# Attention, a capacity-bound top-k and eight experts on one core: the start, the number lookups and the rounds put in other places

## The chip, the cores and the metric

One Trainium2 chip, of which one core is used. The metric is the device time of one execution in microseconds (us). A profile is one more execution, with its instructions and transfers recorded; its span is a little under its time. In the profile PE (or TensorE) does matrix products and transpositions, PEld its weight loads, DVE is VectorE, ACT is ScalarE, POOL is GpSimd, and SP only issues transfers (DMA). "SPq" marks such an issue.

## The reference

```python
q_n, k_n = rmsnorm(q, g_q), rmsnorm(k, g_k)          # 8 batches, 12 heads, 448 tokens, 64 wide
attn = softmax(q_n @ k_n.T / 8)
x = (attn @ v), heads side by side                    # 3584 tokens x 768
logits = x @ w_gate                                   # 8 experts
expert_idx = argmax(logits); gate_w = softmax(logits) at expert_idx
for e in range(8):
    tok_idx = tokens of expert e, the 80 with the largest gate_w
    out[tok_idx] = gate_w[tok_idx] * (relu(x[tok_idx] @ w1[e]) @ w2[e])   # 768 -> 1024 -> 768
```

All other rows of `out` are zero.

## The kernel before

**Pairs.** The work of attention goes by pairs of heads: 6 pairs a batch, 48 in all. One loop runs n from -4 to 51 (L437), and each engine executes its instructions in the order in which this loop issues them. In round n, pair n+4 is loaded on SP (`load_qk`; its 3 buffers are free again when the pair before in the buffer has been normalised), pair n+3 is squared on ScalarE and summed on VectorE, and POOL raises the mean to the power -0.5 (`square`, `rstd`), pair n+2 is multiplied by it (`normalise`, on POOL), pair n+1 is transposed (`transp`), pair n's scores and their exponentials are made (`score`), pair n-1 gets its product with v and the sums of its probabilities on VectorE (`av`, `presum`), pair n-2 is stored as rows of x in DRAM (`xout`, xr_scratch). "Pair n" below stands for "round n of this loop". Every third pair a part of the expert weights is fetched or put into DRAM as bf16 by POOL's queue (`fetch_w1`, `stage_w`, wb_scratch).

**Gate.** When a batch is done, its logits are turned (`gate1` to `gate3`, pairs 6b+7 and 6b+8), and each expert's best 80 tokens are sought by `rounds`: ten rounds of three VectorE instructions (the eight largest, their places, and their removal). This is done in three lists and a last one: batches 0 to 3 together (queued at pair 27), then these with batches 4 and 5 (pair 39), then with batch 6 (pair 45), and batch 7 after the loop. `lists` stores the candidates' token numbers in a table in DRAM (tab_scratch), and `numbers` looks up, for the 80 that stay, which tokens they were: `place` makes table positions on POOL and has TensorE transpose them, `fetch` looks up 80 numbers for one expert by an indirect DMA on POOL, 8 times, and `store` writes the 640 numbers back into the table for the next list.

**The background queue.** Rounds, lists and lookups of a batch are entries with a cost in one list, `queue`; at the end of each pair `work` takes entries until a budget of 4.2 is used up:

```python
def work(us):
    while queue and us > 0:
        cost, f = queue.pop(0)
        f()
        us -= cost
...
return ([(0.3, place)] + [(0.5, lambda e=e: fetch(e)) for e in range(E)]
        + [(0.0, store)])
```

A round costs 1.9 (448 columns), 1.5 (320), 1.2 (240) or 2.1 (528) there.

**The end.** Behind the loop the weights of experts 4 and 5 are loaded (L502), batch 7's ten rounds run, the four results are merged (L510 to L529; `old` reads the numbers of the third list), and for each expert its 80 rows are gathered (`gather`, POOL, three ahead), scaled and transposed (`xpose`), multiplied by both weights and scattered into `out` (L591).

**The start.** Ahead of the first load, SP issues four loads of the norms' weights and six of the gate's (L74, L75, L91).

Of the kernel before, what the change touches and what calls it, by code (L numbers as in the profile page):

```python
# [9 lines left out]
F32 = mybir.dt.float32  # L10
BF16 = mybir.dt.bfloat16
AF = mybir.ActivationFunctionType
# [8 lines left out]
def kernel(  # L21
# [13 lines left out]
    nc = tc.nc  # L35
# [30 lines left out]

    ident = cpool.tile([128, 128], F32, name="ident")
# [5 lines left out]
    for half in range(2):  # L73
        nc.sync.dma_start(out=gk2[half * D:(half + 1) * D, 0:1], in_=g_q[:, None])  # L74
        nc.sync.dma_start(out=gk2[half * D:(half + 1) * D, 1:2], in_=g_k[:, None])  # L75
# [13 lines left out]
    for hh in range(2):  # L89
        for i in range(NG):  # L90
            nc.sync.dma_start(  # L91
                out=wgs[hh * D:(hh + 1) * D, 4 * i + hh:4 * i + hh + 3:2, 8 * i:8 * i + 8],
                in_=wg_v[hh, :, i])
# [21 lines left out]
    nc.sync.dma_start(out=tab_dram[:, 2, CAP:], in_=cand["c"][:, CAP:].bitcast(U32))  # L115
# [36 lines left out]
    with tc.tile_pool(name="qk", bufs=3) as qkpool, \  # L152
# [44 lines left out]
        def normalise(n, a):  # L197
            if a == 0:
                st[n]["qn"] = prep.tile([ST, 2, NT, 2, D], F32, tag="qn", name="qn")
            qk, rs, qn = st[n]["qk"], st[n]["rs"], st[n]["qn"]  # L200
            nc.gpsimd.tensor_mul(  # L201
                qn[:, a].rearrange("p j h d -> p h j d"),
                qk[:, a].rearrange("p h (j d) -> p h j d", d=D),
                rs[:, a].unsqueeze(3).to_broadcast([ST, 2, NT, D]))
# [165 lines left out]
        def numbers(idx, lev, res):  # L370

            add = tpool.tile([CAP, E], U32, tag="add", name="add")

            def place():
                pf = tpool.tile([E, CAP], F32, tag="pf", name="pf")
                nc.gpsimd.tensor_scalar(pf[:, :], idx[:, :], tabF[:, :], float(lev * LT),
                                        op0=ALU.add, op1=ALU.add)
                tp = tpps.tile([128, 512], F32, tag="tp", name="tpn")
                nc.tensor.transpose(tp[:CAP, :E], pf[:, :], ident[:E, :E])
                nc.vector.tensor_copy(add[:, :], tp[:CAP, :E])  # L380
# [7 lines left out]
            def store():  # L388
                if lev < 2:
                    nc.sync.dma_start(out=tab_dram[:, lev + 1, :CAP].rearrange("e s -> s e"),  # L390
                                      in_=res[:, :])
            return ([(0.3, place)] + [(0.5, lambda e=e: fetch(e)) for e in range(E)]
                    + [(0.0, store)])
# [28 lines left out]
        bg[3] += r + numbers(i, 0, num3)  # L422
# [3 lines left out]
        bg[5] += r + numbers(i, 1, num5)  # L426
        r, i = rounds(lambda: cand["c"][:, :], E, LT, best)
        bg[6] = r + numbers(i, 2, num6)
        queue = []

        def work(us):
            while queue and us > 0:
                cost, f = queue.pop(0)
                f()
                us -= cost

        for n in range(-4, NP + 4):  # L437
            if ok(n + 4):
                load_qk(n + 4)
            if ok(n + 2):  # L440
                load_v(n + 2)
            if 4 <= n < 4 + N // 128:
                i = n - 4
                nc.sync.dma_start(out=out[i * 128:(i + 1) * 128, :], in_=zeros[:, :])
# [47 lines left out]
            work(4.2)  # L492
# [10 lines left out]


    v7 = tpool.tile([E, CAP], F32, name="v7")
    last, lidx = rounds(lambda: gst[B - 1]["R"], E, S, v7)
    for cost, f in last:
        f()
    fin = tpool.tile([E, 3, CAP], F32, name="fin")
# [21 lines left out]
    xgs, xts = {}, {}  # L531

    def gather(e):
        xg = mpool.tile([CAP, XW], F32, tag="xg", name="xg", bufs=3)
        nc.gpsimd.memset(xg[:, :], 0.0)
# [24 lines left out]
    for e in range(E):  # L560
# [28 lines left out]
        if e + 3 < E:  # L589
            gather(e + 3)  # L590
# [40 lines left out]
```

## Time and profile before

| | us |
|---|---|
| median of 3 runs (595.93 to 596.67) | 596.28 |
| the profiled execution | 595.21 |
| its span | 593.3 |
| PE busy in it | 496.1 (84%) |
| DVE busy | 379.5 (64%) |
| POOL busy | 354.4 (60%) |
| ACT busy | 322.3 (54%) |

The shares are means over stages that differ: the start, pairs without and with rounds beside them, the last list, and the experts. What bounds a stage is read from the timeline of that stage and from the waits in it. In a timeline row the first number is the start in us from the beginning of the span, the second the time from the first to the end of the last of its x instructions; in brackets stands how long the engine had been idle and what it waited for.

### The profile page before, as it was taken

Reading aid. Unit: us, or ns where it says so; the run is one execution under the profiler, and the core shown is the slowest. Engines: PE = TensorE matmul, PEld = TensorE weight load, DVE = VectorE, ACT = ScalarE, POOL = GpSimd, SP = SyncE. Lnnn points to the kernel's source line nnn. Section 1 sums busy time; section 2 is a strip of 40 time slices with the busy share of each in tenths; the row PEclk is TensorE's granted clock in tenths of the full one; section 3 lists DMA queues with packets and bytes.
Section 4 is the critical chain, followed back from the end, with each engine's and each line's share of the span. In section 5 each row is a group of like instructions: output and inputs, shape, how many; then the busy total and the mean of one; then the engine's idle time right before and its main releaser. Section 6 shows DMA issues by size and latency. Waiting matters only on the chain. (4 is left out here: it accounts for less than half of the span.)

```text
span 593.3 us, 8594 instructions
## 1 busy us (share of the span) xinstructions
PE 496.1 (84%) x3110; PEld 217.9 (37%) x3110; DVE 379.5 (64%) x644; ACT 322.3 (54%) x457; POOL 354.4 (60%) x285
## 2 busy tenths in 40 slices
PE   0699999999999999999987699399997995005795
PEld 0334344434343443344433233144432432004673
DVE  2375647544654555478979952258979999793442
ACT  1577676776677676777745553466663662000110
POOL 1999956877588488564644787347465570324341
PEclk9999999999999999999997979699997998556998
DMA  4339788795969697977947608958654519834931
GB/s 109 95 94 215 187 229 160 214 216 161 257 159 254 145 251 170 255 155 220 206 149 156 152 21 99 146 102 194 151 129 105 112 34 136 310 132 151 379 116 50
DMA packets 84761, 97.55 MB, mean 164 GB/s; under 512 B 11240, under 2 KB 73200, under 8 KB 83696
## 3 DMA queue, kind: packets, MB, share of 16 engines
q1 hardware_dynamic: 68336, 67.88, 39.7%
q0 software_dynamic: 16384, 29.14, 28.1%
q8 instruction: 24, 0.39, 0.3%
q14 instruction: 17, 0.14, 0.1%
HBM read 97.97 MB, written 36.78 MB: 227 GB/s over the span
## 5 line engine op out<-in xcount | busy, mean ns | idle before, releaser
L228 ACT ACTIVATE at<-ps 112x896 f32<-112x896 f32 x192 | 166.4, 918 | 63.0 <-PE ps L224 43.0
L224 PE MATMUL ps<-qkT 64*112 64x448 f32 x768 | 177.1, 582 | 2.8 <-ACT at L228 2.1
L234 PE MATMUL po<-at,vt 112*64 112x448 f32 x768 | 168.2, 560 | 0.1
L193 POOL TENSOR_TENSOR rs<-ms,nhalf 112x16 f32<-112x16 f32 x48 | 143.7, 2994 | 4.0
L190 POOL TENSOR_SCALAR ms<-ssq 112x16 f32<-112x16 f32 x48 | 26.8, 557 | 150.7 <-DVE ssq L187 149.8
L201 POOL TENSOR_TENSOR qn<-qk,rs 112x512 f32<-112x512 f32 x96 | 112.2, 1196 | 2.7
L187 DVE TENSOR_REDUCE ssq<-sq 112x16 f32<-112x1024 f32 x48 | 58.3, 1215 | 81.5 <-ACT sq L181 78.8
L234 PEld LDWEIGHTS po<-at,vt 112*64 112x64 f32 x768 | 47.5, 138 | 112.3 <-issue 102.7
L224 PEld LDWEIGHTS ps<-qkT 64*112 64x112 f32 x768 | 62.7, 178 | 61.0 <-issue 36.6
L244 DVE TENSOR_TENSOR t<-at 112x896 f32<-112x896 f32 x48 | 53.0, 1105 | 30.4 <-ACT at L228 30.3
L209 PE MATMUL tp<-ident,qn 112*128 112x112 f32 x384 | 49.4, 272 | 20.0 <-POOL qn L201 19.3
L181 ACT ACTIVATE sq<-qk 112x1024 f32<-112x1024 f32 x48 | 50.7, 1057 | 27.2 <-DMA qk<-in_k_dram 24.6
L245 DVE TENSOR_TENSOR sm<-sm,t 112x896 f32<-112x896 f32 x48 | 59.0, 1228 | 1.6
L209 PEld LDWEIGHTS tp<-ident,qn 112*128 112x128 f32 x384 | 38.5, 144 | 55.3 <-POOL qn L201 34.6
L214 ACT ACTIVATE qkT<-tp,gqk 128x448 f32<-128x448 f32 x48 | 30.3, 631 | 43.5 <-PE tp L209 38.8
L243 DVE TENSOR_TENSOR sm<-at 112x896 f32<-112x896 f32 x48 | 53.4, 1112 | 0.0
L572 ACT ACTIVATE h_sb<-ph 128x320 bf16<-128x320 f32 x16 | 6.9, 437 | 72.8 <-PE ph L568 72.8
L250 ACT COPY us<-po 128x448 f32<-128x448 f32 x48 | 25.7, 534 | 25.4 <-PE po L234 24.7
L399 PE MATMUL xp<-ident,us 128*112 128x128 f32 x192 | 31.6, 288 | 8.8 <-ACT qkT L214 8.8
L399 PEld LDWEIGHTS xp<-ident,us 128*112 128x112 f32 x192 | 19.7, 135 | 42.7 <-ACT at L228 24.7
L402 ACT COPY xb<-xp 112x512 f32<-112x512 f32 x48 | 28.5, 593 | 10.2 <-DMA xr_scratch<-xb 7.5
L383 POOL DMA_INDIRECT num<-tab_scratch,add x24 | 26.9, 1121 | 8.9 <-issue 5.7
(96 smaller groups left out, 392.3 us busy)
## 6 DMA issues: line engine op xcount, KB each, us to landing
w_sb<-in_moe_w_dram POOLq DMA_DIRECT2D x8, 1536.0 KB
wb_scratch<-in_moe_w_dram POOLq DMA_DIRECT2D x8, 1536.0 KB
w_sb<-wb_scratch SPq DMA_DIRECT2D x8, 1536.0 KB, 9.6
qk<-in_q_dram SPq DMA_DIRECT2D x48, 224.0 KB, 7.2
qk<-in_k_dram SPq DMA_DIRECT2D x48, 224.0 KB, 6.0
vt<-in_v_dram SPq DMA_DIRECT2D x48, 224.0 KB, 4.0
xr_scratch<-xb SPq DMA_DIRECT2D x48, 224.0 KB, 3.5
out_dram<-zeros SPq DMA_DIRECT2D x28, 384.0 KB, 5.0
```

The source lines that it names most:

```text
L181: nc.scalar.activation(sq[:, :], st[n]["qk"][:].rearrange("p a h x -> p (a h x)"), AF.Square)
L187: nc.vector.reduce_sum(out=ssq[:, :], in_=st[n]["sq"][:].rearrange("p (g d) -> p g d", d=D), axis=AX.X)
L193: nc.gpsimd.tensor_tensor(rs[:].rearrange("p a h j -> p (a h j)"), ms[:, :], nhalf[:, :], op=ALU.pow)
L201: nc.gpsimd.tensor_mul(qn[:, a].rearrange("p j h d -> p h j d"), qk[:, a].rearrange("p h (j d) -> p h j d", d=D), rs[:, a].unsqueeze(3).to ...
L209: nc.tensor.transpose(tp[:, j * ST:(j + 1) * ST], st[n]["qn"][:, a, j].rearrange("p h d -> p (h d)"), ident[:ST, :ST])
L224: nc.tensor.matmul(ps[:, hh, :S], st[n]["T1"][hh * D:(hh + 1) * D, j * ST:(j + 1) * ST], st[n]["T0"][hh * D:(hh + 1) * D, :], start=True, ...
L228: nc.scalar.activation(st[n]["at%d" % (j // 2)][:, j % 2], ps[:, :, :S], AF.Exp)
L234: nc.tensor.matmul(st[n]["po"][hh * D:(hh + 1) * D, :S], st[n]["v"][:, hh, j * D:(j + 1) * D], st[n]["at%d" % (j // 2)][:, j % 2, hh, :], ...
L243: nc.vector.tensor_add(sm[:], a0[:, 0], a0[:, 1])
L244: nc.vector.tensor_add(t1[:], a1[:, 0], a1[:, 1])
L245: nc.vector.tensor_add(sm[:], sm[:], t1[:])
L399: nc.tensor.transpose(xp[:ST, j * 128:(j + 1) * 128], st[n]["us"][:, j * ST:(j + 1) * ST], ident[:, :])
```

## The change

Five edits.

- The first loads of q and k stand at the head of SP's queue. The norms' weights are loaded by ScalarE's queue, the gate's weights behind the loads of pair 0's round, the table's constant part in pair 5. A tiny exponential ahead of everything makes ScalarE load its table at once.
- The two multiplies of `normalise` run on VectorE for pairs 0 to 2.
- `numbers` goes into a second queue. `place` keeps only POOL's step; `turn` (transposition and copy) and the lookups, two at a time, are entries with a stop behind each, so that `work` does one of them a pair.
- The budget of `work` depends on the pair: 0.8 where a batch's gate is evaluated, 3.0 in the pair before, 3.8 otherwise.
- The three first gathered tiles are cleared ahead of the last rounds, later ones aren't cleared again; `gather(e + 3)` stands ahead of expert e's second product in the code, and the output tile has three buffers.

```diff
+    warm = cpool.tile([1, 2], F32, name="warm")
+    nc.vector.memset(warm[:, :], 0.0)
+    nc.scalar.activation(warm[:, 0:1], warm[:, 1:2], AF.Exp)
...
-        nc.sync.dma_start(out=gk2[half * D:(half + 1) * D, 0:1], in_=g_q[:, None])
-        nc.sync.dma_start(out=gk2[half * D:(half + 1) * D, 1:2], in_=g_k[:, None])
+        nc.scalar.dma_start(out=gk2[half * D:(half + 1) * D, 0:1], in_=g_q[:, None])
+        nc.scalar.dma_start(out=gk2[half * D:(half + 1) * D, 1:2], in_=g_k[:, None])
...
-            nc.gpsimd.tensor_mul(
+            eng = nc.vector if n < 3 else nc.gpsimd
+            eng.tensor_mul(
...
             def place():
-                pf = tpool.tile([E, CAP], F32, tag="pf", name="pf")
                 nc.gpsimd.tensor_scalar(pf[:, :], idx[:, :], tabF[:, :], float(lev * LT),
                                         op0=ALU.add, op1=ALU.add)
+
+            def turn():
                 tp = tpps.tile([128, 512], F32, tag="tp", name="tpn")
...
-            return ([(0.3, place)] + [(0.5, lambda e=e: fetch(e)) for e in range(E)]
-                    + [(0.0, store)])
+            stop = (99.0, lambda: None)
+            todo = [(0.0, place), stop, (0.3, turn), stop]
+            for e in range(E):
+                todo.append((0.0, lambda e=e: fetch(e)))
+                if e % 2 == 1:
+                    todo.append(stop)
+            return todo + [(0.0, store)]
...
+        for b in nums:
+            bg[b].append((0.0, lambda b=b: queue2.extend(nums[b])))
+        queue, queue2 = [], []
 
         def work(us):
-            while queue and us > 0:
-                cost, f = queue.pop(0)
-                f()
-                us -= cost
+            for qq, t in ((queue, us), (queue2, 1.0)):
+                while qq and t > 0:
+                    cost, f = qq.pop(0)
+                    f()
+                    t -= cost
...
+            if n == 0:
+                load_wgs()
+            if n == 5:
+                nc.sync.dma_start(out=tab_dram[:, 2, CAP:],
+                                  in_=cand["c"][:, CAP:].bitcast(U32))
...
-            work(4.2)
+            work(0.8 if n >= 8 and n % 6 == 2 else 3.0 if n % 6 == 1 else 3.8)
...
+    xgs, xts = {}, {}
+    for e in range(3):
+        xgs[e] = mpool.tile([CAP, XW], F32, tag="xg", name="xg", bufs=3)
+        nc.gpsimd.memset(xgs[e][:, :], 0.0)
+    work(1)
...
     for cost, f in last:
         f()
+        work(1)
+    while queue2:
+        work(1)
...
+        if e + 3 < E:
+            gather(e + 3)
         DN = DM // 2
-        yo = mpool.tile([CAP, DM], F32, tag="yo", name="yo")
+        yo = mpool.tile([CAP, DM], F32, tag="yo", name="yo", bufs=3)
...
-        if e + 3 < E:
-            gather(e + 3)
```

Three places in the order of the instructions. A row is a line of the kernel, the operation, what it writes and reads, and how often it stands there in a row.

The start on VectorE, before (ssq is the sum of squares of a pair, gqk the product of the norms' weights):

```order
L97 MEMSET zeros 128x768
L77 TENSOR_TENSOR gqk<-gk_65 128x1
L78 TENSOR_SCALAR gqk<-gqk 128x1
L109 CAST tabF<-tabI 8x1
L70 CAST identb<-ident 128x128
L187 TENSOR_REDUCE ssq<-sq 112x16 x4
L243 TENSOR_TENSOR sm<-at 112x896
```

and now (qn is the normalised pair):

```order
L103 MEMSET zeros 128x768
L192 TENSOR_REDUCE ssq<-sq 112x16
L80 TENSOR_TENSOR gqk<-gk_68 128x1
L81 TENSOR_SCALAR gqk<-gqk 128x1
L115 CAST tabF<-tabI 8x1
L73 CAST identb<-ident 128x128
L207 TENSOR_TENSOR qn<-qk,rs 112x2x4x64 x2
L192 TENSOR_REDUCE ssq<-sq 112x16
L207 TENSOR_TENSOR qn<-qk,rs 112x2x4x64 x2
L192 TENSOR_REDUCE ssq<-sq 112x16
```

The first sum now stands ahead of the small constants, and the multiplies of pairs 0 to 2 stand between the sums.

POOL at the first list's lookups, before (pf are the table positions, num the numbers that are looked up; ms and rs are mean and power, qn the multiplies):

```order
L376 TENSOR_SCALAR pf<-idx,tabF 8x80
L383 DMA num_157<-tab_scratch,add 80x1 x2
L201 TENSOR_TENSOR qn<-qk,rs 112x2x4x64 x2
L190 TENSOR_SCALAR ms<-ssq 112x16
L193 TENSOR_TENSOR rs<-ms,nhalf 112x16
L383 DMA num_157<-tab_scratch,add 80x1 x6
L136 DMA wb_scratch<-in_moe_w_dram 1024x1x768
```

and now:

```order
L383 TENSOR_SCALAR pf<-idx,tabF 8x80
L141 DMA wb_scratch<-in_moe_w_dram 1024x1x768
L207 TENSOR_TENSOR qn<-qk,rs 112x2x4x64 x2
L195 TENSOR_SCALAR ms<-ssq 112x16
L198 TENSOR_TENSOR rs<-ms,nhalf 112x16
L207 TENSOR_TENSOR qn<-qk,rs 112x2x4x64 x2
L195 TENSOR_SCALAR ms<-ssq 112x16
L198 TENSOR_TENSOR rs<-ms,nhalf 112x16
L392 DMA num_153<-tab_scratch,add 80x1 x2
```

The lookups, which were issued two and then six at a time, follow the positions two pairs later and go two a pair.

SP at the end of attention, before (rz goes to x's table with the last batch's gate, w_sb are the weights of experts 4 to 7, num_158 the numbers of the second list):

```order
L403 DMA xr_scratch<-xb 448x1x128 x2
L390 DMA tab_scratch<-num_158 80x8x1
L403 DMA xr_scratch<-xb 448x1x128 x3
L296 DMA xr_scratch<-rz 448x1x12
L141 DMA w_sb<-wb_scratch 128x6144 x8
```

and now:

```order
L417 DMA xr_scratch<-xb 448x1x128 x5
L302 DMA xr_scratch<-rz 448x1x12
L146 DMA w_sb<-wb_scratch 128x6144 x4
L399 DMA tab_scratch<-num_154 80x8x1
L146 DMA w_sb<-wb_scratch 128x6144 x4
```

The store of the second list's numbers stood ahead of three stores of x and of all weights; now it stands behind the weights of experts 4 and 5.

## Rows read from the trace of the kernel before

**Rows 1.** Windows: length, busy PE, PEld, DVE, ACT, POOL, then PE clock, DMA share, GB/s.

```profile
100.00:200.00 100.00, 100.00 (x586) 40.55 (x582) 53.60 (x58) 71.80 (x101) 74.10 (x50) 1.00 0.84 208
...
490.00:520.00 30.00, 9.06 (x57) 3.62 (x53) 26.52 (x64) 3.11 (x7) 5.73 (x7) 0.69 0.97 230
```

**Rows 2.** Timeline of the start, all engines: start, length, engine, line, operation.

```profile
0.75 0.59 SPq L74 DMA_DIRECT2D gk<-in_g_q_dram  x1
...
7.23 0.59 SPq L166 DMA_DIRECT2D qk<-in_q_dram  x1
...
11.22 1.28 ACT L181 ACT_TABLE_LOAD   x1 [11.22 <-DMA qk<-in_k_dram]
...
13.60 1.22 DVE L187 TENSOR_REDUCE ssq<-sq 112x16 f32<-112x1024 f32 x1 [8.01 <-ACT sq L181]
...
15.20 2.93 POOL L193 TENSOR_TENSOR rs<-ms,nhalf 112x16 f32<-112x16 f32 x1
...
18.22 2.04 POOL L201 TENSOR_TENSOR qn<-qk,rs 112x512 f32<-112x512 f32 x2
...
21.95 3.33 PE L224 MATMUL ps<-qkT 64*112 64x448 f32 x8 [0.62 <-ACT qkT L216]
...
28.42 1.08 DVE L243 TENSOR_TENSOR sm<-at 112x896 f32<-112x896 f32 x1
```

**Rows 3.** Timeline of TensorE, pairs 31 to 37.

```profile
314.46 1.07 PE L278 MATMUL zt<-ident,zsb 128*112 128x128 f32 x4 [4.24 <-ACT xb L402]
...
341.86 0.23 PE L379 MATMUL tpn<-ident,pf 8*80 8x8 f32 x1 [5.88 <-POOL pf L376]
342.02 3.33 PE L224 MATMUL ps<-qkT 64*112 64x448 f32 x8
345.28 2.88 PE L234 MATMUL po<-at,vt 112*64 112x448 f32 x8
...
349.00 1.76 PE L224 MATMUL ps<-qkT 64*112 64x448 f32 x8
350.69 1.73 PE L234 MATMUL po<-at,vt 112*64 112x448 f32 x8
...
379.80 1.10 PE L399 MATMUL xp<-ident,us 128*112 128x128 f32 x4 [8.77 <-ACT qkT L214]
381.04 3.33 PE L224 MATMUL ps<-qkT 64*112 64x448 f32 x8
```

**Rows 4.** Timeline of SP and of ScalarE, pairs 35 and 36.

```profile
361.35 0.31 SPq L390 DMA_DIRECT2D tab_scratch<-num  x1
...
378.17 1.06 ACT L181 ACTIVATE sq<-qk 112x1024 f32<-112x1024 f32 x1 [11.58 <-DMA qk<-in_k_dram]
```

**Rows 5.** DMA issues: engine, count, KB of one, median us to landing.

```profile
tab_scratch<-num SPq DMA_DIRECT2D x8, 2.5 KB, 16.1
```

**Rows 6.** Line L403, the 48 stores of x.

```profile
DMA to landing us min/median/max: 2.8/3.5/10.3
```

**Rows 7.** Timeline of VectorE, between the third and the last list.

```profile
512.86 0.16 DVE L380 CAST add<-tpn 80x8 uint32<-80x8 f32 x1 [1.07 <-PE tpn L379]
```

**Rows 8.** Timeline of SP and of POOL at the last list: weights, first and last lookup.

```profile
506.91 45.88 SPq L141 DMA_DIRECT2D w_sb<-wb_scratch  x8
...
513.31 1.01 POOL L383 DMA_INDIRECT num<-tab_scratch,add  x1 [0.77 <-DVE add L380]
...
521.93 0.91 POOL L383 DMA_INDIRECT num<-tab_scratch,add  x1 [0.30 <-issue]
```

**Rows 9.** Windows of 2 us at the weights' end (columns as in rows 1).

```profile
524.00:526.00 2.00, 0.00 (x0) 0.00 (x0) 1.90 (x6) 0.00 (x0) 0.00 (x0) 0.50 0.11 31
```

**Rows 10.** Tile old: duration min, median, max in ns, first and last start.

```profile
L521 DVE CAST old<-num x1: 168/168/168, 533.4 to 533.4; 80x8 f32<-80x8 uint32 x1
```

**Rows 11.** Timeline of POOL and of TensorE, the last experts.

```profile
571.64 0.78 POOL L535 MEMSET xg<- 80x780 f32 x1
...
579.29 0.39 PE L551 MATMUL pxt<-identb,xn 80*128 80x80 bf16 x6 [1.12 <-DVE xn L545]
```

More of the change, by code (lines that the diff above doesn't have):

```diff
@@ L88, with load_wgs @@
     wg_v = moe_w_gate.rearrange("(i c hh d) e -> hh d i c e", hh=2, c=2, d=D)
[L89 to L93, printed above, removed]
+    def load_wgs():
+        for hh in range(2):
+            for i in range(NG):
+                nc.sync.dma_start(
+                    out=wgs[hh * D:(hh + 1) * D, 4 * i + hh:4 * i + hh + 3:2, 8 * i:8 * i + 8],
+                    in_=wg_v[hh, :, i])
     nhalf = cpool.tile([ST, 16], F32, name="nhalf")
@@ L114 @@
     nc.gpsimd.iota(tok6, pattern=[[1, S]], base=6 * S, channel_multiplier=0)
-    nc.sync.dma_start(out=tab_dram[:, 2, CAP:], in_=cand["c"][:, CAP:].bitcast(U32))
     wpool = ctx.enter_context(tc.tile_pool(name="moe_w", bufs=1))
@@ L372, in numbers @@
             add = tpool.tile([CAP, E], U32, tag="add", name="add")
+            pf = tpool.tile([E, CAP], F32, tag="pf", name="pf")
             def place():
-                pf = tpool.tile([E, CAP], F32, tag="pf", name="pf")
                 nc.gpsimd.tensor_scalar(pf[:, :], idx[:, :], tabF[:, :], float(lev * LT),
                                         op0=ALU.add, op1=ALU.add)
+            def turn():
                 tp = tpps.tile([128, 512], F32, tag="tp", name="tpn")
@@ L421 @@
         r, i = rounds(lambda: cand["a"][:, :], E, 4 * CAP, cand["b"])
-        bg[3] += r + numbers(i, 0, num3)
+        bg[3] += r
+        nums = {3: numbers(i, 0, num3)}
         r, i = rounds(lambda: gst[5]["R"], 64, S, v45)
@@ L425 @@
         r, i = rounds(lambda: cand["b"][:, :], E, 3 * CAP, cand["c"])
-        bg[5] += r + numbers(i, 1, num5)
+        bg[5] += r
+        nums[5] = numbers(i, 1, num5)
         r, i = rounds(lambda: cand["c"][:, :], E, LT, best)
-        bg[6] = r + numbers(i, 2, num6)
-        queue = []
-        def work(us):
-            while queue and us > 0:
-                cost, f = queue.pop(0)
-                f()
-                us -= cost
+        bg[6] = r
+        nums[6] = numbers(i, 2, num6)
+        for b in nums:
+            bg[b].append((0.0, lambda b=b: queue2.extend(nums[b])))
+        queue, queue2 = [], []
+        def work(us):
+            for qq, t in ((queue, us), (queue2, 1.0)):
[3 more added lines that the diff above has]
+                    t -= cost
         for n in range(-4, NP + 4):
@@ L529 @@
     nc.vector.tensor_add(idxT[:, :], new[:, :], bad[:, :])
-    xgs, xts = {}, {}
     def gather(e):
-        xg = mpool.tile([CAP, XW], F32, tag="xg", name="xg", bufs=3)
-        nc.gpsimd.memset(xg[:, :], 0.0)
+        xg = xgs.get(e)
+        if xg is None:
+            xg = mpool.tile([CAP, XW], F32, tag="xg", name="xg", bufs=3)
         nc.gpsimd.indirect_dma_start(
```

## The prediction

> **What bounds the kernel now.** I read the windows view by stage first. Through the middle TensorE is busy 100 of 100 us at the full clock; around the end of attention VectorE takes its place with 26.52 of 30 us, and TensorE has only 9.06 [rows 1]. So a microsecond saved counts where TensorE stands still on the way into the full stretch or inside it, and where VectorE's chain or what follows it ends late. Second, the timeline of the start: TensorE gets its first scores at 21.95, behind a single chain of load, square, sum, power, multiply and transposition [rows 2]. Third, TensorE's timeline around pairs 33 to 37: it waits twice, 5.88 and 8.77 us, and runs at half speed after each [rows 3]. Fourth, what stands behind the second wait: a store of candidate numbers and a late k load [rows 4, 5]. Fifth, the end of attention and the start of the experts [rows 6 to 11].
>
> **Start.** The first q load leaves SP at 7.23, behind ten loads of constants of which the first left at 0.75; the change puts q there: 7.23 - 0.75 = 6.5 us [rows 2]. The table load, which waits for that k load and takes 1.28 us, now runs on ScalarE before the data come: 1.3 us [rows 2]. ScalarE issues four small loads too; at 0.59 us each, the nearest row, and with the table load they take 3.6 us from 0.75 on, which ends at about 4.4 and so before k (it landed 11.22 - 7.23 = 4.0 us after q's issue): nothing. The two multiplies that make qn took POOL 2.04 us [rows 2]. VectorE has none of this shape in the trace; its nearest row is an addition of 896 columns in 1.08 us, so 512 columns make about 0.65 and two 1.3: a gain of 0.7; bounds 0 (as slow as POOL) and 1.0. Sum 8.5; I take **-8.4**, bounds -7.7 to -8.8. Pairs 1 and 2 don't lose it again: VectorE's queue now holds sum, multiplies, sum, multiplies in turn, so a pair costs 1.22 + 0.38 (from the sum's end to the power) + 2.93 + 1.3 = 5.8 us [rows 2]. That is 0.4 over POOL's 0.38 + 2.93 + 2.04, 0.8 for both, and TensorE has pair 0's scores to work on meanwhile. The gate weights' six loads now stand on SP between two loads of pairs that wait for a free buffer anyway, and the table's constant part is stored at pair 5; both hidden.
>
> **The first wait, pair 33.** Today POOL turns the indices into table positions at the end of pair 33 and TensorE's transposition of them stands behind that at once: 5.88 us [rows 3]. After it the scores take 3.33 us for 1.76 and the next groups 2.88 for 1.73: 2.7 us more [rows 3]. In the new order POOL's step is issued in pair 34 and the transposition at the end of pair 35, a whole pair later, so TensorE finds it done. What would be late next is VectorE, which sums the probabilities behind the rounds; the new budgets give it one round in pair 32 instead of three, and the rounds that are left run in pairs 33 and 34, beside full matmuls. **-8.6**; bounds -6 (VectorE's lag holds the scores) and -8.6.
>
> **The second wait, pair 36.** The eight lookups and the store behind them sit on POOL and SP in one go. The store goes out at 361.35, with the loads of a pair queued behind it; ScalarE then waits 11.58 us for k, until 378.17 [rows 4], and TensorE 8.77, with scores of 3.33 instead of 1.76 behind it [rows 3]: 10.3 us. Now two lookups a pair run in pairs 36 to 39, and the store is issued at pair 40, when they landed long before. The loads of pairs 39 to 44 go out on time. **-10.3**; it comes back in part if the store slows the loads of pair 45 in the same way, since it takes 16.1 us to land [rows 5] and a weight transfer is issued at about the same time. There VectorE is the later engine (it runs rounds without a break then), so a few microseconds of ScalarE's lie under it: **+0.5**, bounds 0 and 10.3.
>
> **The end of attention.** The ten rounds of each list are the same instructions in the same total; from pair 43 on only their places differ, and VectorE works through them without gaps in both orders: 0. The transposed positions of the last list no longer hold VectorE between lists, 1.07 us [rows 7]; but the copy of the second list's now stands in pair 47, behind a transposition that TensorE issues last in its pair: 0 to 1.1 by the same row, I take **+0.5**. The first saving is only worth something if nothing else ends later, and something does.
>
> That is the **store of the second list's numbers**. Before, it was on SP ahead of batch 7's stores; now it is behind four weight loads of 1.5 MB, and the eight lookups of the last list need it in the table. Today the weights go out at 506.91 and are all in at 524.2 (of the window from 524 the transfer engines are busy 0.11) [rows 8, 9]. SP's queue shows what lies behind another transfer: a store of x takes 3.5 us at the median but up to 10.3, and I take the latter to be one that stood behind a number store [rows 5, 6]. Whether a small store passes large loads no row shows, so the bounds are 2.8 us after its issue (the fastest store in [rows 6], which hides it) and 16.1 after the weights' end. I take it to land 2.8 after that end, at 527.0. From the first lookup's start to the eighth's is 521.93 - 513.31 = 8.6 us [rows 8], and 2.8 for the last to land: 538.4, against 533.4, when VectorE reads the numbers now [rows 10]: +5.0. Without the older store in front, SP may issue the weights up to some 2 us earlier; half of that makes **+4.0**, bounds 0 and 17.
>
> The Trainium skill, page "DMA: Bandwidth & Descriptors", section "Queues, rings and completion order", says that on each transfer engine the descriptors of one queue are consumed in ring order, and that the engine alternates only between queues. By that the store can't pass the weights, and the sum would hold +4.0 or more and never 0; the slow store of x agrees, but no row here shows a small store behind weights.
>
> **The experts.** The clearing of the gathered tiles goes away behind the third gather: 0.78 us each [rows 11]. Most of it is covered by the weights that are being loaded and by TensorE's work; at the last transposition TensorE waits 1.12 for a gather that the clearing held up [rows 11]: **-1.1** in all, bounds 0 and -3 (three or four such clearings in a row). The order of POOL is still gather 4 behind scatter 0, gather 5 behind scatter 1, so the move in the code by itself gives 0; the third output buffer takes a wait of VectorE that lies beside the wait for the gathers: 0.
>
> **Sum.** -8.4 - 8.6 - 10.3 + 0.5 + 0.5 + 4.0 - 1.1 = -23.4. The profiled execution took 595.2 us, 1.1 under the median of 596.3, so 571.8 in a profile and **572.9 us** as a median.
>
> **Rivals.** (a) The small store passes the weights: the +4.0 falls away, 568.9. For it: 2.5 KB against 6 MB [rows 5]; against it the 10.3 us of [rows 6]. (b) The store of pair 40 stalls the loads as that of pair 36 did: 10.3 comes back in place of the 0.5, 582.7. For it: weights are staged at the same place; against it VectorE's longer queue there, and loads that are no longer late beforehand. (c) The last store takes its 16.1 us even with the weights gone: 524.2 + 16.1 - 1.0 + 8.6 + 2.8 = 550.7, 17.3 above 533.4 instead of 4.0: 586.2. (d) **Slower:** one mechanism, the store of 640 single numbers, with a landing time s at both its places. At pair 40 it gives the 10.3 back and s - 16.1 more; at the end it costs 524.2 - 1.0 + s + 8.6 + 2.8 - 533.4 = s + 1.2. With the rest (-8.4 - 8.6 + 0.5 - 1.1 = -17.6) that is 2s - 32.5: nothing is gained at s of 16.3, and at 20 us it is 7.5 slower, 603.8. Against it: the measured 16.1 had q, k, v and staged weights around it. (e) Another wait follows at once where pair 33's went (VectorE's rounds up to pair 33, or POOL's copies between two lists): 8 of the 18.9 us stay, 580.9. For it: TensorE waits 4.24 at the end of pair 31 today, behind VectorE's lag [rows 3], and pairs 27 to 31 keep their rounds.
>
> **How the numbers follow.** Forecast 0.55, with 567 to 577 by its own bounds; (a) 0.16; (b) 0.12; (e) 0.08; (c) 0.05; (d) 0.03 slower and 0.01 the same. The range 564.5 to 581 holds the forecast, (a) and (e), and leaves out most of (b), (c) and (d). About 0.2% is what this kernel's measurement can tell: faster 0.96, same 0.01, slower 0.03.
>
> **What would show it.** First scores at 13 to 14 us. TensorE without a wait of over 1 us between pairs 33 and 37 and at full clock there; a wait of some 4 us in pair 31 as before. SP's number store issued just behind four weight loads, the first lookup of the last list starting only after the weights are in, and VectorE's read of those numbers waiting for the last lookup. A first lookup that starts while the weights still move is (a); ScalarE waiting over 8 us for k of pair 45 is (b). The forecast is wrong in kind if the first scores come later than 16 us, or if TensorE's waits between pairs 31 and 45 still add up to more than 20 us.

## The result, and the profile after

The changed kernel takes **571.54 us** (median of 4 runs, 571.14 to 571.95), the kernel before 596.13 beside it; ratio 0.9586, 95% interval 0.957 to 0.9603. The forecast was 572.9 with 564.5 to 581. The profiled span went from 593.3 to 569.7, by 23.6, where the sum had 23.4. How far the same instruction moved shows where it came from (the last column adds up the prediction's terms; xp is the transposition of a pair's x ahead of its store, ft that of the merged results, pxt that of an expert's gathered rows):

| instruction | before | after | moved | predicted |
|---|---|---|---|---|
| TensorE, first scores | 21.95 | 15.02 | -6.9 | -8.4 |
| xp of pair 27 | 272.44 | 265.96 | -6.5 | -8.4 |
| xp of pair 34 | 352.35 | 336.84 | -15.5 | -17.0 |
| xp of pair 37 | 392.28 | 364.82 | -27.5 | -27.3 |
| ft, the merging of the lists | 533.33 | 504.75 | -28.6 | -26.3 |
| VectorE reads the last numbers (old) | 533.44 | 512.08 | -21.4 | -22.3 |
| first expert's transposes (pxt) | 540.00 | 518.69 | -21.3 | |
| end of the span | 593.3 | 569.7 | -23.6 | -23.4 |

The rows of ft and of the first pxt, first before, then now (start, duration, engine, line; in brackets the idle time and its releaser):

```profile
533.33 0.40 PE L515 MATMUL ft<-ident,fin 8*80 8x8 f32 x3 [20.50 <-DVE fin L511]
540.00 0.58 PE L551 MATMUL pxt<-identb,xn 80*128 80x80 bf16 x6 [6.27 <-DVE xn L545]
...
504.75 0.40 PE L549 MATMUL ft<-ident,fin 8*80 8x8 f32 x3 [19.28 <-DVE fin L545]
518.69 0.58 PE L584 MATMUL pxt<-identb,xn 80*128 80x80 bf16 x6 [13.53 <-DVE xn L578]
```

So the sum met the span within 0.2 us and the forecast the median within 1.4, made of a start that gave too little, waits that gave a little more, and a late store that took back more.

The engines' busy time and shares on the page of the profile after: TensorE has 8.2 us less than before, VectorE 4.5 more.

```profile
PE 487.9 (86%) x3110; PEld 215.8 (38%) x3110; DVE 384.0 (67%) x651; ACT 322.9 (57%) x458; POOL 344.0 (60%) x274
```

The timeline of the start (start, duration, engine, line, idle time and releaser), which answers to [rows 2]:

```profile
11.25 1.76 PE L215 MATMUL tp<-ident,qn 112*128 112x112 f32 x8 [11.25 <-DVE qn L207]
...
11.71 1.22 DVE L192 TENSOR_REDUCE ssq<-sq 112x16 f32<-112x1024 f32 x1
...
12.96 1.06 ACT L186 ACTIVATE sq<-qk 112x1024 f32<-112x1024 f32 x1 [4.71 <-DVE ssq L192]
13.93 0.62 ACT L220 ACTIVATE qkT<-tp,gqk 128x448 f32<-128x448 f32 x1
...
15.02 3.33 PE L230 MATMUL ps<-qkT 64*112 64x448 f32 x8 [2.01 <-ACT qkT L222]
```

The transposes are through at 13.0, 8.3 us earlier than before (21.3). But their evictions, which the first scores wait for, stand on ScalarE behind a square that waits 4.71 us for VectorE's second sum, and 1.4 of the 8.3 are lost there.

TensorE in pairs 31 to 37, against [rows 3]:

```profile
307.79 1.07 PE L284 MATMUL zt<-ident,zsb 128*112 128x128 f32 x4 [4.22 <-ACT xb L416]
...
318.82 0.65 PE L413 MATMUL xp<-ident,us 128*112 128x128 f32 x4
...
346.67 0.65 PE L413 MATMUL xp<-ident,us 128*112 128x128 f32 x4
347.25 0.20 PE L388 MATMUL tpn<-ident,pf 8*80 8x8 f32 x1
354.99 0.65 PE L413 MATMUL xp<-ident,us 128*112 128x128 f32 x4
```

The wait of pair 31 is as it was; the two behind it (5.88 and 8.77) have no row any more: tpn follows xp at once.

The second list's store behind the four weight loads: SP, POOL and VectorE in the timeline, then windows (busy time of the engines, granted clock, share and speed of the transfer engines), against [rows 8 to 10]:

```profile
476.68 2.32 SPq L146 DMA_DIRECT2D w_sb<-wb_scratch  x4
479.29 0.32 SPq L399 DMA_DIRECT2D tab_scratch<-num  x1
...
500.61 0.98 POOL L392 DMA_INDIRECT num<-tab_scratch,add  x1 [15.43 <-DVE idx L356]
...
509.21 0.91 POOL L392 DMA_INDIRECT num<-tab_scratch,add  x1 [0.30 <-issue]
...
512.08 0.17 DVE L555 CAST old<-num 80x8 f32<-80x8 uint32 x1 [7.22 <-DMA num<-tab_scratch,add]
```

```profile
492.00:494.00 2.00, 0.00 (x0) 0.00 (x0) 1.91 (x5) 0.00 (x0) 0.00 (x0) 0.50 0.91 351
494.00:496.00 2.00, 0.00 (x0) 0.00 (x0) 1.90 (x6) 0.00 (x0) 0.00 (x0) 0.50 0.13 13
496.00:500.00 4.00, 0.00 (x0) 0.00 (x0) 3.79 (x11) 0.00 (x0) 0.00 (x0) 0.50 0.00 0
```

The weights are in at about 494.2 and the transfer engines stand still from 496 on, yet the first lookup starts at 500.61. (Its idle time is put down to VectorE's idx, which was done at 484; what came last was the store.) VectorE, done with its rounds, waits 7.22 us.

The experts. The last scatter before and VectorE's write of its data (yo); then, now, POOL's first scatter, TensorE's one long wait, and the same two rows:

```profile
587.41 0.61 DVE L584 TENSOR_SCALAR yo<-py,gwT 80x384 f32<-80x384 f32 x1 [0.69 <-PE py L581]
588.30 0.91 POOL L591 DMA_INDIRECT out_dram<-yo,idxT  x1 [4.02 <-DVE yo L584]
...
526.80 1.44 POOL L624 DMA_INDIRECT out_dram<-yo,idxT  x1 [6.95 <-DVE yo L619]
...
539.75 0.49 PE L584 MATMUL pxt<-identb,xn 80*128 80x80 bf16 x6 [3.03 <-DVE xn L578]
...
563.16 0.61 DVE L619 TENSOR_SCALAR yo<-py,gwT 80x384 f32<-80x384 f32 x1 [0.69 <-PE py L616]
564.72 0.91 POOL L624 DMA_INDIRECT out_dram<-yo,idxT  x1 [3.03 <-DVE yo L619]
```

### The profile page after: what moved, and what is told of

Same layout as the page of the kernel before. It is cut to its first block, busy times and chain, and to the rows that moved or that the text cites. A ratio compares the mean times of both kernels' runs of the same rounds, so it can differ in the third digit from the quotient of the medians.

```text
span 569.7 us, 8586 instructions
## 1 busy us (share of the span) xinstructions
PE 487.9 (86%) x3110; PEld 215.8 (38%) x3110; DVE 384.0 (67%) x651; ACT 322.9 (57%) x458; POOL 344.0 (60%) x274
## 3 DMA queue, kind: packets, MB, share of 16 engines
q0 software_dynamic: 16384, 29.14, 28.6%
## 5 line engine op out<-in xcount | busy, mean ns | idle before, releaser
L230 PE MATMUL ps<-qkT 64*112 64x448 f32 x768 | 174.1, 573 | 3.6 <-ACT qkT L222 2.0
L240 PE MATMUL po<-at,vt 112*64 112x448 f32 x768 | 165.3, 552 | 0.0
L207 POOL TENSOR_TENSOR qn<-qk,rs 112x512 f32<-112x512 f32 x90 | 105.8, 1203 | 2.4
L195 POOL TENSOR_SCALAR ms<-ssq 112x16 f32<-112x16 f32 x48 | 29.2, 608 | 127.9 <-DVE ssq L192 122.5
L392 POOL DMA_INDIRECT num<-tab_scratch,add x24 | 24.1, 1003 | 34.1 <-DVE idx L356 15.4
## 6 DMA issues: line engine op xcount, KB each, us to landing
wb_scratch<-in_moe_w_dram POOLq DMA_DIRECT2D x8, 1536.0 KB, 12.5
```

The lines of the kernel that those rows point to most:

```text
L207: eng.tensor_mul(qn[:, a].rearrange("p j h d -> p h j d"), qk[:, a].rearrange("p h (j d) -> p h j d", d=D), rs[:, a].unsqueeze(3).to_broad ...
L230: nc.tensor.matmul(ps[:, hh, :S], st[n]["T1"][hh * D:(hh + 1) * D, j * ST:(j + 1) * ST], st[n]["T0"][hh * D:(hh + 1) * D, :], start=True, ...
L240: nc.tensor.matmul(st[n]["po"][hh * D:(hh + 1) * D, :S], st[n]["v"][:, hh, j * D:(j + 1) * D], st[n]["at%d" % (j // 2)][:, j % 2, hh, :], ...
```

## Experiments

Twelve kernels ran. All but start_alone start from the changed kernel (571.5 us).

| run | median us | ratio to before, 95% interval |
|---|---|---|
| store_ahead | 565.57 | 0.9499 (0.9468 to 0.9529) |
| reduce_ahead | 571.00 | 0.9579 (0.9551 to 0.9606) |
| pool_multiplies | 570.87 | 0.9587 (0.9559 to 0.9615) |
| budget_42 | 565.75 | 0.9502 (0.9475 to 0.9529) |
| start_alone (from before) | 587.73 | 0.9869 (0.983 to 0.9909) |
| turn_at_once | 579.35 | 0.9733 (0.9694 to 0.9772) |
| lookups_at_once | 578.40 | 0.9714 (0.9675 to 0.9753) |
| experts_old | 572.58 | 0.9625 (0.9595 to 0.9654) |
| lists_stop | 562.93 | 0.9468 (0.9441 to 0.9494) |
| gathers_six | 570.77 | 0.9592 (0.9569 to 0.9615) |
| all_mends | 560.87 | 0.9423 (0.9398 to 0.9449) |
| stores_aside | 556.71 | 0.9361 (0.9341 to 0.9381) |

The kernel before took 594.5 to 596.1 us beside these groups of runs, so a difference of two medians from different groups can be off by up to 1.7 us. Where that matters, the difference of the ratios (a hundredth is 6.0 us) is given too.

### The late store: store_ahead

The new line issues the store of the second list's numbers.

```diff
+    queue2.pop(0)[1]()
     for e in range(NW0, NW0 + 2):
         load_weights(wlate, e, e)
         fetch_late(e)
```

> The changed kernel, with the store of the second list's numbers issued just ahead of the four late weight loads instead of behind them. Theory: that store is what keeps the last list's lookups waiting (first one at 500.61 with 15.43 us of idle before it, their addresses cast at 486.39) and so VectorE 7.22 us at its read of the numbers. Then the first lookup starts at 486.5 to 489, the last has landed by 500, VectorE reads the numbers without a wait at about 505, and the time falls by 7 us, to 564.5 us (564 to 566). Rival: with the weights moving, the lookups themselves crawl, or the experts wait for the weights anyway; then the wait only changes its name and the time falls by under 2 us (569.5 or more).

6.0 us less (5.2 by the ratios). Its timeline of SP, POOL and TensorE:

```profile
475.49 0.36 SPq L399 DMA_DIRECT2D tab_scratch<-num  x1
...
485.67 0.97 POOL L392 DMA_INDIRECT num<-tab_scratch,add  x1 [1.63 <-DVE add L389]
...
494.25 0.91 POOL L392 DMA_INDIRECT num<-tab_scratch,add  x1 [0.31 <-issue]
...
503.59 0.40 PE L550 MATMUL ft<-ident,fin 8*80 8x8 f32 x3 [19.27 <-DVE fin L546]
510.74 0.58 PE L585 MATMUL pxt<-identb,xn 80*128 80x80 bf16 x6 [6.75 <-DVE xn L579]
```

The lookups start as soon as their addresses are there, with the weights moving (409 to 434 GB/s), 8.58 us from the first to the eighth as against 8.60 in the profile after, and from ft to the first pxt it is 7.15 us instead of 13.94. The rival (lookups that crawl) is out: the whole wait came from the store's place in SP's queue.

### The budgets: budget_42

```diff
-            work(0.8 if n >= 8 and n % 6 == 2 else 3.0 if n % 6 == 1 else 3.8)
+            work(4.2)
```

> The changed kernel, with the same 4.2 of rounds after each pair as the kernel before had, in place of 0.8, 3.0 and 3.8. The list of steps then runs ahead: the second list's store falls ahead of the late weight loads by itself, and the first list's lookups and store fall one pair earlier. Theory: the spreading with its own stops removed the two waits, the budgets did not; they only pushed the second store behind the weights. Then the waits of pairs 33 and 36 stay away, VectorE's wait for the last lookups goes (-7 us), some of it is given back where rounds crowd a pair (0 to 4 us): 564.5 to 568.5. Rival: the budgets are what keeps TensorE from waiting in pairs 31 to 37; then a TensorE wait of over 4 us comes back there and the time is 571 or more.

5.8 us less (5.0 by the ratios), and TensorE has no wait of over 1 us between pairs 32 and 41. So the budgets by pair did not remove the two waits. What they did was to let the queue run late enough for the store to fall behind the weights; with the old budget it goes out at 479.65, ahead of the first weights at 480.29. (Further on it has waits of 3.10 us at 423.04 and 3.36 at 430.90, where the changed kernel has 1.09 and 1.20.)

### The two waits: turn_at_once and lookups_at_once

Both edits change the first list (lev 0) alone.

```diff
-            todo = [(0.0, place), stop, (0.3, turn), stop]
+            todo = [(0.0, place), (0.3, turn), stop] if lev == 0 else [
+                (0.0, place), stop, (0.3, turn), stop]
```

> The changed kernel, with the first list's transpose of addresses put in the same turn as its place on POOL, without a stop between (the lookups then start one pair earlier too). Theory: this stop alone removed the first wait: TensorE now waits in pair 33 or 34 for POOL's place, which waits for VectorE's last round, as in the kernel before (8.6 us with what trails); time up by 5 to 9 us on the changed kernel, 576.5 to 580.5. Rival: the wait was made by the lists running late under the old budgets; TensorE waits under 2 us and the time stays under 573.5.

7.8 us more (8.8 by the ratios). TensorE, with the half-speed scores behind the wait:

```profile
340.71 0.23 PE L388 MATMUL tpn<-ident,pf 8*80 8x8 f32 x1 [3.92 <-POOL pf L383]
340.87 3.33 PE L230 MATMUL ps<-qkT 64*112 64x448 f32 x8
344.13 2.91 PE L240 MATMUL po<-at,vt 112*64 112x448 f32 x8
```

It is the first wait of [rows 3] again, a pair later: 3.92 us, and 16.7 from the xp of pair 34 (336.14) to the next (352.88), where the changed kernel needs 9.8.

```diff
-                if e % 2 == 1:
+                if e % 2 == 1 and lev > 0:
                     todo.append(stop)
```

> The changed kernel, with the first list's eight lookups in one turn instead of two a pair, and its store right behind them, three pairs earlier on SP's queue. Theory: spreading removed the second wait. Eight lookups at 1.22 us hold POOL for 9.7 us (2.4 in the spread turns), so the next multiplies come 7.3 us later, and the store on SP waits for the last to land and holds back the loads of the next pairs; TensorE waits again around pairs 35 to 38, 5 to 11 us: time 576.5 to 582.5. Rival: POOL and SP have a pair's slack (POOL is busy 60% of the span) and swallow it: under 2 us, below 573.5.

6.9 us more (7.6 by the ratios). SP, ScalarE and TensorE:

```profile
348.76 0.50 SPq L173 DMA_DIRECT2D qk<-in_k_dram  x1
367.40 0.31 SPq L399 DMA_DIRECT2D tab_scratch<-num  x1
...
377.83 1.06 ACT L186 ACTIVATE sq<-qk 112x1024 f32<-112x1024 f32 x1 [9.52 <-DMA qk<-in_k_dram]
...
379.47 1.10 PE L413 MATMUL xp<-ident,us 128*112 128x128 f32 x4 [6.43 <-ACT qkT L220]
```

That is the second wait [rows 3, 4] in the same form: a store on SP that waits for eight lookups, no load of q or k between 349 and 367, ScalarE without k, TensorE without transposes. Each of the two kinds of stop removes one wait; neither removes the other's. (6.9 of the 11.95 us that this stretch gained come back; what holds the rest was not separated. In the kernel before a staged weight of 1.5 MB, wb_scratch, left POOL at 359.89, ahead of the store, and k was missed for 15.9 us after its issue; here none left ahead of it, and it was missed for 9.5.)

### The start: start_alone, reduce_ahead, pool_multiplies

start_alone has the first edit's lines and the multiplies on VectorE in the kernel before, and nothing else.

> The kernel before with the start of the change alone: warm-up activation, g_q and g_k on ScalarE's queue, gate weights and list constants loaded later, the first three pairs' multiplies on VectorE. Theory: the start is worth what the trace of the changed kernel shows at pair 27 (265.96 against 272.44), 6.5 us, and the two waits of pairs 33 and 36 simply come 6.5 us sooner: ratio to before 0.989 (588.9 to 590.0). Rival: part of it is swallowed by the waits further on, whose releasers (store, lookups) keep their own time; then less than 4 us (ratio above 0.993).

The ratio is worth 7.8 us, with an interval of 5.4 to 10.1; its trace stands 7.3 earlier at pair 27 (265.19) and 6.4 at the first expert. Nothing is swallowed on the way. The profiles of the changed kernel, store_ahead, budget_42 and experts_old, with the same start, have that xp at 265.28 to 265.96: it is worth 6.5 to 7.3.

```diff
+            if n < 0 and ok(n + 3):
+                rstd(n + 3)
             if ok(n + 2):
                 normalise(n + 2, 0)
...
-            if ok(n + 3):
+            if n >= 0 and ok(n + 3):
                 rstd(n + 3)
```

> The changed kernel, with the sums of squares of pairs 1 and 2 on VectorE ahead of the multiplies of the pair before. Theory: the start gained 6.9 us and not 8.4 because the second sum stood behind the first multiplies (11.71 instead of about 8), so the third square on ScalarE (one buffer) came at 12.96 and held up the two evictions of the first transposes; with the order turned the third square is done by 9.5, the evictions start as soon as the transposes are through (about 12.5), first scores at 13.3 to 13.7, and the time falls by 1.2 to 1.6 us (570.0 to 570.4). Rival: TensorE is held later in the first pairs by the rs of pairs 1 and 2 on POOL (2.9 us each), so first scores move but the end doesn't: within 0.4 us of 571.5.

First scores at 13.20, as expected, and 2.3 us earlier at pair 27 (263.70); but the end is where it was. Neither theory had the place where it was lost. TensorE in the experts:

```profile
516.32 0.58 PE L586 MATMUL pxt<-identb,xn 80*128 80x80 bf16 x6 [13.05 <-DVE xn L580]
...
520.95 3.65 PE L618 MATMUL py<-w_sb,h_sb 128*80 128x384 bf16 x16
```

The first pxt is still 2.4 earlier than 518.69. Then the first expert's second product takes 3.65 instead of 2.77 (TensorE comes out of its idle time at the 1.2 GHz level), and the scatters, 1.3 earlier at first (525.53), are 0.1 earlier at last (564.62): the loss is in the experts, not in the first pairs. Of it 1.1 lies ahead of the first scatter and 1.2 in the distances between the scatters, which bound this stretch (gathers_six); why these got longer was not separated.

```diff
-            eng = nc.vector if n < 3 else nc.gpsimd
-            eng.tensor_mul(
+            nc.gpsimd.tensor_mul(
```

> The changed kernel, with the first three pairs' multiplies back on POOL. Theory: my sum gave 0.7 us for their move to VectorE (2.04 against 1.3); but on VectorE they also push the second sum of squares back, and with them on POOL that sum runs at about 8.3, so the square is out of the evictions' way: first scores at about 14.2 (15.02 now). From there POOL has rs and multiplies in one row (5 us a pair, against TensorE's 6.7 to 7.6), which still keeps up. Time 0 to 1 us less, 570.5 to 571.5. Rival, the sum as I predicted it: 0.7 us more, 572.2, and first scores at 15.7 or later.

First scores at 13.86, 1.2 us earlier than with the multiplies on VectorE, and no change of the time that can be told. The 0.7 that I gave for this move doesn't reach the first scores: what VectorE saves in the multiplies (1.29 against 2.04) is lost because the next sum stands behind them.

### The experts: experts_old, gathers_six

```diff
             xg = mpool.tile([CAP, XW], F32, tag="xg", name="xg", bufs=3)
+            nc.gpsimd.memset(xg[:, :], 0.0)
...
-        yo = mpool.tile([CAP, DM], F32, tag="yo", name="yo", bufs=3)
+        yo = mpool.tile([CAP, DM], F32, tag="yo", name="yo")
```

> The changed kernel, with the experts' part as before in two things: a memset ahead of each later gather again, and two buffers for the experts' outputs instead of three. Theory: these two gave the 2.3 us by which the stretch from the first expert's transposes to the end got shorter (53.3 to 51.0): the fifth gather starts 2.1 us later behind its memset, and time goes up by 1 to 2.5 us, to 572.5 to 574.0. Rival: the stretch differs by itself from run to run by that much (the clock's rise and the late weights meet it at other points): no change, within 0.5 us of 571.5.

1.0 us more at the median, 2.3 by the ratios, whose intervals just touch, and 0.5 in the profile from the first pxt to the end (51.5 for 51.0). (The 2.1 us in the expectation are a misread row of three memsets; one takes 0.75.) The rival isn't out: that stretch took 51.0 in the profile after and 53.3 in that of reduce_ahead with the same code there, and with the old code 53.3 in the profile before and 52.3 in that of start_alone. So what these two edits hold of the 2.3 is not shown.

```diff
+    for e in range(3, 6):
+        xgs[e] = mpool.tile([CAP, XW], F32, tag="xg", name="xg", bufs=6)
+        nc.gpsimd.memset(xgs[e][:, :], 0.0)
...
-    for e in range(3):
+    for e in range(6):
         gather(e)
...
-        if e + 3 < E:
-            gather(e + 3)
+        if e + 6 < E:
+            gather(e + 6)
```

> The changed kernel, with six buffers for the gathered rows, six gathers issued at once and the seventh and eighth as buffers come free, so that the fifth no longer stands behind the first scatter on POOL and behind the late weights' traffic. Theory: the TensorE waits in the experts (3.03 us at 539.75, 0.48 at 546.61, and the slow products behind the first) go, and the time falls by 3 to 4.5 us on the changed kernel: 567.0 to 568.5. Rival: the experts then run into the loads of the last two experts' weights, which land at about 543 whatever the order, or the six gathers slow the first one: under 1.5 us, 570 or more.

The expected effect came, and the time stayed, as the rival had it but not for its reason alone. The wait of 3.03 is gone, and TensorE's last product starts at 555.60 instead of 560.29. The end is set elsewhere. POOL and TensorE at the end of this run:

```profile
526.25 1.44 POOL L627 DMA_INDIRECT out_dram<-yo,idxT  x1 [3.20 <-DVE yo L622]
...
536.51 0.95 POOL L627 DMA_INDIRECT out_dram<-yo,idxT  x1 [7.54 <-DVE xn L581]
545.13 0.93 POOL L627 DMA_INDIRECT out_dram<-yo,idxT  x1 [7.67 <-DVE yo L622]
548.88 0.91 POOL L627 DMA_INDIRECT out_dram<-yo,idxT  x1 [2.82 <-DVE yo L622]
...
555.60 2.84 PE L619 MATMUL py<-w_sb,h_sb 128*80 128x384 bf16 x16
...
564.05 0.91 POOL L627 DMA_INDIRECT out_dram<-yo,idxT  x1 [2.83 <-DMA out_dram<-yo,idxT]
```

The eight scatters go one after the other; the last is released by the landing of the one before, though its data were ready at 559.1. They stand 3.7 to 3.9 us apart, but 10.3 and 8.6 while the last two experts' weights come in. From the first to the last it is 37.8 here, 37.9 in the profile after, 39.5 before, and 5 us more to the end. This chain bounds the experts here: TensorE gained 4.7 us and the last scatter 0.7. In the changed kernel TensorE's path comes out close behind: the last scatter's data are ready at 563.77, 0.95 ahead of it. In the kernel before they were ready at 588.0 and the scatter left 0.3 later, released by them.

### The lists, and all together: lists_stop, all_mends, stores_aside

```diff
-            return [(0.0, go)]
+            return [(0.0, go), (99.0, lambda: None)]
```

> The changed kernel, with a stop behind each step that copies a list on POOL, so that the next rounds on VectorE come after the next pair's own work. The steps then fall so that the second list's store stands ahead of the late weight loads, as in store_ahead; so this run is held against that one (565.6 us). Theory: VectorE's idle times for the copies (3.58 us at 300.65, 3.04 at 416.74) hold the sums of pairs 30 and 42 and with them TensorE (4.22 us at 307.79); with the stop VectorE does the pair's sums while POOL copies, TensorE's wait goes, and the time is 3 to 7 us under store_ahead's: 558.5 to 562.5. Rival: VectorE is full in pairs 30 to 33 and again from 41 on, so the rounds come later by what was saved and the wait comes back at the next transposes: within 2 us of store_ahead, 563.5 or more.

2.6 us under store_ahead (1.8 by the ratios, whose intervals overlap): between the two theories, and near the rival. The wait of 4.22 in pair 31 is gone, and pair 32 stands 6.4 us earlier than in store_ahead (311.26 against 317.64). At ft 2.1 are left (501.46 against 503.59): TensorE waits 3.0 at 416.14, for a k that was missed for 14.8 us after its issue behind the first list's store, and VectorE is the later engine at the end.

all_mends puts the edits of lists_stop, reduce_ahead and gathers_six together.

> The changed kernel with the stop behind the list copies (which also puts the second store ahead of the weights), the sums of squares ahead of the multiplies at the start, and six gathers at once. If the parts add up: 571.5 less 6 for the store, 0.5 to 2 for the start, 3 to 4.5 for the gathers, 0 to 7 for the lists: 552 to 562 us; most likely 558. If TensorE's or VectorE's own work at the end sets the bound (the last rounds on VectorE, 21 us), the lists and the start give little and it stays at 561 or more.

560.87: inside the range, above the likeliest. One wait had grown. POOL, SP, ScalarE and TensorE from pair 41 on (wb_scratch is the staged weight):

```profile
395.01 0.97 POOL L141 DMA_DIRECT2D wb_scratch<-in_moe_w_dram  x1
396.62 0.32 SPq L399 DMA_DIRECT2D tab_scratch<-num  x1
398.08 0.31 SPq L171 DMA_DIRECT2D qk<-in_q_dram  x1
398.45 0.68 SPq L173 DMA_DIRECT2D qk<-in_k_dram  x1
...
415.16 1.06 ACT L186 ACTIVATE sq<-qk 112x1024 f32<-112x1024 f32 x1 [9.60 <-DMA qk<-in_k_dram]
416.79 1.10 PE L413 MATMUL xp<-ident,us 128*112 128x128 f32 x4 [4.90 <-ACT qkT L220]
```

The k load behind the store of 640 single numbers is missed until 415, 16.7 us after its issue: rival (b) of the prediction, which stayed away in the changed kernel (there the store landed in 7.8 us and ScalarE waited 3.14). One more thing differs, and no run changed it alone: here a staged weight left ahead of the store and of k, in the changed kernel behind both (at 399.82; k at 397.50).

stores_aside, as a difference to all_mends; `put` holds a list's stores, which were part of `go`:

```diff
-                    nc.sync.dma_start(
+                    (nc.scalar if lev == 0 else nc.sync).dma_start(
...
-            return todo + [(0.0, store)]
+            return todo + ([stop] if lev == 0 else []) + [(0.0, store)]
...
-            return [(0.0, go), (99.0, lambda: None)]
+            return [(0.0, go), (99.0, lambda: None), (0.0, put)]
```

> The kernel of all_mends, with the first list's store of numbers on ScalarE's queue one pair later, so that no load stands behind it, and the second list's two stores one pair later on SP's, behind no wait for POOL's copies. In all_mends that store (396.62) and these two (409.87, SP held for 5.9 us) stood ahead of the loads of k: ScalarE waited 9.60 us for one at 415.16, TensorE 4.9 us at 416.79. Theory: it was the order in the queue; on another queue the store takes its time beside the loads, the two waits go, and the time falls by 4 to 5.5 us on all_mends (560.9): 555.5 to 557. Rival: the store's small pieces slow every transfer wherever they are queued, or the loads are late for another reason; then ScalarE's wait for k stays over 5 us and the time above 559.5.

4.2 us less again (3.7 by the ratios):

```profile
398.02 0.54 SPq L173 DMA_DIRECT2D qk<-in_k_dram  x1
...
402.47 0.37 ACTq L403 DMA_DIRECT2D tab_scratch<-num  x1
...
409.60 1.06 ACT L186 ACTIVATE sq<-qk 112x1024 f32<-112x1024 f32 x1 [4.49 <-DMA qk<-in_k_dram]
```

The k that ScalarE waits for left 4.45 us ahead of the store and is there 11.6 us after its issue, where it took 16.7 in all_mends; ScalarE waits 4.49 instead of 9.60, and TensorE's xp of this pair has no wait. So having the store ahead of it cost this k about 5 us, and the rest of its delay is there without one. The kernel before has the like at 256.17: a k load that left 1.7 us behind a staged weight, with no number store issued yet, landed after 12.4 us. The run moves the store to another queue and behind this k in one, and the second list's two stores as well; what each gave was not separated. At **556.71 us** this is the fastest version: 6.4% under the kernel before, 2.3% under the changed one by the ratios.

The Trainium skill, page "DMA: Bandwidth & Descriptors", section "Queues, rings and completion order", has each transfer engine take a queue's descriptors in ring order and alternate between queues; it promises no order of completion over the engines together, which is less than the prediction's "can't pass". The trace agrees with the first half: behind four weight loads the store was not in before them (first lookup 500.61, weights in at 494.2). No run here shows the second: in stores_aside the k in question left ahead of the store.

## Why the prediction was right, step by step

- **Start, predicted -8.4, measured -6.5 to -7.3.** The mechanism (q ahead of ten loads, the table early) held; the term was too large: what came lies outside its own bounds, -7.7 to -8.8, and the first scores came at 15.02, not at 13 to 14. The failed part is "a gain of 0.7" for the multiplies on VectorE, with its queue read as "sum, multiplies, sum, multiplies in turn" and priced for pairs 1 and 2 alone. That order also holds pair 0: the second sum at 11.71 keeps the only buffer of the squares, and the third square keeps ScalarE from the evictions (8.3 us gained at the end of the transposes, 6.9 at the first scores). Turning the order gives 1.8 at the first scores (reduce_ahead), leaving the multiplies on POOL 1.2.
- **First wait, -8.6, measured -8.8** (15.5 - 6.7, the shift in pair 33). The stop between POOL's step and the transposition does it: turn_at_once gives 7.8 to 8.8 back.
- **Second wait, -10.3, measured -11.95** (27.46 - 15.51). Right in kind: lookups_at_once brings the store, the late k and TensorE's wait back. A staged weight ran beside the store, which the prediction names in (b) and (d) but not here; a k beside such a transfer was late without a store as well (12.4 and 11.6 us, see stores_aside). The slow stretch behind the wait was put too small: the xp of pair 36 moved by 9.3, and pair 37, 12.5 us before and 9.8 now, gave 2.65 more.
- **Store at pair 40, +0.5, and copy at pair 47, +0.5, measured 0.1 together** (27.46 to 27.35): ScalarE waits 3.14 for k at 408.18 and TensorE 0.54 behind it. That such a store can cost was right too: 4.9 us of TensorE in all_mends.
- **VectorE between lists, not in the sum**: the 1.07 us of [rows 7] are gained: from zt of batch 7 to ft the shift goes from 27.35 to 28.6.
- **Store behind the weights, +4.0, measured +7.2** (the shift falls from 28.6 at ft to 21.4 at old). The order in the queue was right, and (a), a store that passes, is out. The mis-sized part is "2.8 after that end": from the end of the weights at 494.2 to the first lookup it took 6.4, 3.6 more, the last 4 of it with idle transfer engines. The 8.6 for eight lookups and the 2.8 to the last landing came as taken (500.61, 509.21, 512.08), and the weights went out 1.65 earlier against ft where 1.0 was taken. What holds the lookup in these 4 us no run shows. (c), 16.1 us, is out too. One of the prediction's reasons was misread: the store of x that took 10.3 us left between 145 and 155 us, long before the first number store (361.35), so it was no sign of a store held behind another.
- **Experts, -1.1, measured -2.3.** Mis-sized, and its reason holds in part. TensorE's wait for a gather was taken to set the end. In the kernel before the last scatter was released by its data, so a TensorE wait could count; in the profile after its data were there 0.95 ahead of it, and with TensorE 4.7 us earlier the chain of scatters is the bound (gathers_six). The first scatter came 0.7 nearer to the first pxt, the chain got 1.6 shorter, 1.0 of it at its last link. That the edits did this is not shown: with the clearing back (experts_old) TensorE's wait of 1.12 at the last transposition does not come back, and start_alone, with the old code, has a chain of 38.1.
- **(e)**, another wait in pairs 31 to 33, did not come: the wait of pair 31 stayed at 4.22, as the list of signs had it.

The errors of the steps, +1.9 (start), -1.9 (the two waits), -0.9 (the two small terms), -1.2 (VectorE between lists), +3.2 (store) and -1.2 (experts), cancel: that the total is nearer than its terms is luck.

## What to carry to other kernels

A store of many small pieces belongs behind nothing large and ahead of nothing urgent: move it to another queue, or ahead of the bulk, before its data are needed (6.0 us in store_ahead; 4.2 in stores_aside, with two other stores moved along). A wait that TensorE shows is worth something only if the chain that ends last runs through it; ask that of the last store of the program too. And an instruction moved to a faster engine takes a place in that engine's queue: look at what now stands behind it, and at the buffers which that one holds.

## What the runs showed of the hardware

- The store of 640 numbers of 4 bytes was short or long by its surroundings: 7.8 us to landing at pair 40 in the changed kernel, 16.1 before [rows 5], and in all_mends the k behind it came 16.7 us after its issue. A k behind such a store with no staged weight ahead of it came after 9.5 us (lookups_at_once), one beside a staged weight with no such store ahead of it after 11.6 (stores_aside) and 12.4 (before). Behind the weights 6.4 us passed until it released a lookup, the last 4 with idle transfer engines.
- Weight loads at full rate did not slow the lookups: 8.58 us for eight in store_ahead, 8.60 with nothing else moving.
- In gathers_six scatters of 80 rows of 3 KB followed each other at 3.7 to 3.9 us alone, at 10.3 and 8.6 beside weight loads.
- After its idle time around the last rounds (granted clock 0.50, the 1.2 GHz level) TensorE's first expert product took 3.28 us for 1.88 later on; in reduce_ahead, where the second product started 2.2 us earlier in time (520.95 against 523.10), it too met the granted clock of 0.50 and took 3.65 for 2.77.
